# Filler matmuls on TensorE while the convolution's matrices are built

## The chip, the cores and the metric

The kernel runs on one core of one Trainium2 chip. Its time is the device time of one execution in microseconds (us), taken as the median over several executions. Five engines work side by side: TensorE (PE in the profile, with its weight loads as PEld), VectorE (DVE), ScalarE (ACT), GpSimd (POOL) and SyncE (SP), which here issues most of the DMAs. Matmul results land in PSUM, eight banks of 2 KB per partition. TensorE's clock is throttled by the chip: the profile shows the granted clock as a share of full speed, and in this kernel it is always either 1.0 or 0.5.

## The reference

Two independent parts are joined on the last axis. Part A is a recurrent memory attention over 64 segments of 32 rows, part B a state-space convolution (S4 form) over 2048 positions and 1024 channels:

```python
a = _A_ref(A_x, A_mem0, A_Wq, A_Wk, A_Wv, A_Wo, A_seg_len)     # 64 segments, one after the other
# part B, for each channel d:
P = jnp.exp(logdA[:, :, None] * l[None, None, :])              # powers of the state, l = 0 .. 2047
K = jnp.einsum('dn,dnl,dn->dl', Cc, P, dB).real                # the convolution's kernel
Kf, Uf = rfft2(pad(K)), rfft2(pad(u))                          # length 4096
y = irfft2(Uf * Kf)[..., :L] + u * Dskip
return jnp.concatenate([a, y], axis=-1)
```

## The kernel before, in words

Part B comes first (roughly the first 590 us), then part A (the remaining 1350 us); loads of part A's weights are already issued during part B. The order of the work is written out by hand (`manual_schedule`): each engine runs its instructions in the order in which the program issues them, and waits only where data or a buffer demand it.

Part B has three stages. First, 16 passes (lines 1325 to 1360) compute samples of the convolution's kernel K, transform u into the frequency domain (kept in DRAM as `Ud`), and make part A's projections. Then comes the stage that the change touches, lines 1367 to 1423 and the blocks 0 to 3 of the loop at line 1526. Last come the blocks 4 to 15 of that loop, with the inverse transforms.

In the touched stage K's spectrum is needed, and for it matrices of cosines and sines are built. There are four of them (`G[kc]`, kc = 0 to 3), each made in 14 steps by the generator `build` (line 1179):

- One step makes the basis: a matmul with 7 rows by 7 columns, moving 512 elements (line 1190), then a sine on ACT.
- Ten steps make angles: two matmuls with 7 rows and 128 columns, 256 elements each, into one bank (line 1186), then a sine of 512 elements per partition on ACT (line 1177).
- Three steps make weights: one matmul with 7 rows and 512 elements (line 1198), then a copy on ACT (line 1199).

Every step takes a PSUM bank (named `gf`) from a pool of three, which the tiles `kp` use too. `make(kc, n)` (line 1369) runs n of the steps. `weighted(kc, n_)` (line 1205) multiplies three of the five angle blocks of one half of `G[kc]` by the weights, on DVE. `spectrum(b, n_)` (line 1217) is 20 matmuls of 128 rows and 128 columns, 256 elements each, into a tile of two banks: `pa` for blocks 0 to 3, `hps` later. `times_u` (line 1377, operation at line 1380) multiplies the spectrum by u's, on DVE, and `rotate` (1383, 1384) ends the complex product. `values(15, t)` (line 1063) are the last small matmuls for K, into two of the three `gf` banks; `table_ops["x"]` (line 1071) copies them out on DVE.

PE's order in the touched stage is: 9 steps of `make(0)`; 3 more; `spectrum(0, 0)`; 2 more; `spectrum(0, 1)`; 9 steps of `make(1)`; `values(15, 0)` and `values(15, 1)`; 5 more steps; `spectrum(1, 0)`; `spectrum(1, 1)`; 14 steps of `make(2)`. Then in block 1 of the loop `spectrum(2, 0)`, 7 steps of `make(3)`, `spectrum(2, 1)` and 7 steps; in block 2 the two halves of `spectrum(3)`; in block 3 those of `spectrum(4)`. At the start of block 3 the PSUM pools are closed and two new ones are opened, `ps_h` for the tiles `hps` and `ps_y` for the tiles `yp` of the inverse transforms. `load_u(b)` (line 1215) issues on SP the two loads `wq<-Ud` for block b; they wait until DVE has read the buffers they overwrite. `inverses` (lines 1506 to 1521) end with a store on ACT's queue, `out_dram<-uu`.

Two other names are needed: `ps_t` (line 998) is the pool of one bank that held the tiles `ptt` of the first stage, and `Dsk` (line 735) is a constant of 128 x 1024 in bf16, loaded in the eighth of the 16 passes (line 1327) and used by DVE at line 1486.

Of the kernel before, what the change touches and what calls it, by code (L numbers as in the profile page):

```python
# [11 lines left out]
F32 = mybir.dt.float32  # L12
# [675 lines left out]

COARSE = [(16, 32, 16), (544, 64, 8), (1088, 128, 8)]
FINE = [(-64, 8, 4), (-32, 4, 4), (-16, 1, 32), (16, 4, 4), (32, 8, 5)]  # L690
TURNS = [(0, 1, 17), (20, 4, 4), (40, 8, 4)]
NC, NP, NN, NA = 32, 25, 24, 25
STEP, CENTER, ONE = 16, 192.0, 120
# [18 lines left out]
def part_b(ctx, tc, u, A_re, A_im, B_re, B_im, C_re, C_im, log_dt, Dskip, out_b, ahead, copies, residents, first_state):  # L712
# [6 lines left out]
    v, sc, gp, pe, sy = nc.vector, nc.scalar, nc.gpsimd, nc.tensor, nc.sync  # L719
# [15 lines left out]
    Dsk = const.tile([128, D], BF16, name="Dsk")  # L735
# [41 lines left out]
    with tc.tile_pool(name="b_par", bufs=1) as par, tc.tile_pool(name="b_parh", bufs=2) as parh, \  # L777
# [35 lines left out]
        o = 0  # L813
        for b0, st, n in FINE + COARSE + TURNS:
            gp.iota(jI[:, o:o + n], pattern=[[st, n]], base=b0, channel_multiplier=0)
# [152 lines left out]
        for word_ in PAR:  # L968
            word = word_.rstrip("/")
            nm, n_ = word[0], word[1:]  # L970
# [27 lines left out]
    ps_t = ctx_p.enter_context(tc.tile_pool(name="b_pst", bufs=1, space=PSUM))  # L998
# [206 lines left out]
    def weighted(kc, n_, amp):  # L1205
        a_ = amp.rearrange("p (j q) -> p j q", j=3)[:, :, 256 * n_:256 * n_ + 256]
        g_ = G[kc][:, n_, 2:5].rearrange("p j s h f -> p j s (h f)")
        v.tensor_tensor(out=g_, in0=g_, in1=a_.unsqueeze(2).to_broadcast([128, 3, 2, 256]), op=ALU.mult)
# [4 lines left out]
    def load_u(b):  # L1213
        for n_ in range(2):
            sy.dma_start(out=uq[n_], in_=Ud[b % 4, b // 4][:, 2 * n_:2 * n_ + 2].rearrange("p a c d -> p (a c d)"))

    def spectrum(b, n_, outs, halves=(0, 1)):
        dq, kc = b // 4, b % 4
        KT = ks[dq // 2]
        d = slice(DQ * (dq % 2), DQ * (dq % 2) + DQ)  # L1220
        for half in halves:
            for cs in range(2):
                for j in range(5):
                    pe.matmul(outs[half][:, cs, :], lhsT=G[kc][:, n_, j, cs, half, :], rhs=KT[j][:, d], start=(j == 0), stop=(j == 4), skip_group_check=True)  # L1224
# [57 lines left out]
    def cosine(r, h):  # L1282
        sc.activation(out=cosines(r, h), in_=T["n", r, h][:], func=ACT.Sin, scale=-TWO_PI, bias=hp[:])

    def minus(r, h):
        wn = T["w", r, h] = tmp.tile([128, 32, NN], BF16, name="wn", tag="wn", bufs=1)
        v.tensor_scalar(out=wn[:], in0=turned(windows(T["s", r, h])), scalar1=-1.0, scalar2=None, op0=ALU.mult)

    def imaginary(r, h):
        products(r, h, "gi", windows(T.pop(("s", r, h))), T.pop(("w", r, h))[:])  # L1290

    def real(r, h):
        c_ = cosines(r, h).rearrange("p (a b) -> p a b", a=32)
        products(r, h, "gr", c_, turned(c_))

    def values(r, t):
        T["K", r, t] = part(r, t, [T["gr", r, h] for h in range(2)], [T["gi", r, h] for h in range(2)])
# [68 lines left out]

    made = [build(kc, lambda: take([128, 512], F32, "gf"), amps[kc]) for kc in range(4)]

    def make(kc, n):
        for _ in range(n):  # L1370
            next(made[kc])

    def halves():
        t_ = ps_e.tile([128, 2, 512], F32, name="pa", tag="pa")
        return [t_[:].rearrange("p h (c d) -> p h c d", c=2)]
# [9 lines left out]
    now = [halves() for _ in range(2)]  # L1385
    first = XT[:, 15360:19456].bitcast(F32).rearrange("p (a b c d) -> p a b c d", a=2, b=2, c=2)
    zs = [up.tile([128, 2, 2, DQ], F32, name="us", tag="us", bufs=3) for n_ in range(2)]
    absolute(15, 0)
    minus(15, 0)
    make(0, 9)  # L1390
    imaginary(15, 0)
    absolute(15, 1)
    minus(15, 1)
    imaginary(15, 1)
    make(0, 3)
    weighted(0, 0, amps[0])
    spectrum(0, 0, [now[0][0][:, half] for half in range(2)])
    make(0, 2)
    weighted(0, 1, amps[0])
    spectrum(0, 1, [now[1][0][:, half] for half in range(2)])  # L1400
    cosine(15, 0)
    cosine(15, 1)
# [3 lines left out]
    load_u(1)  # L1406
    real(15, 1)
    make(1, 9)
    for t in range(2):
        values(15, t)  # L1410
    make(1, 5)
# [40 lines left out]
    def pointwise(b, s_):  # L1452
        kc, Bt = b % 4, Bs[b // 4]
        Y = Yp[:] if b else first
        whole = b > 3
        if b:
            for n_ in range(2):
                times_u(s_, Y[:, n_], Zs[:, n_], n_)
                if n_ == 0 and not whole:
                    rotate(Y[:, n_], Zs[:, n_])  # L1460
        yield
        if whole:
            rotate(Y.rearrange("p n a c d -> p (n a) c d"), Zs[:].rearrange("p n a c d -> p (n a) c d"))
        elif b:
            rotate(Y[:, 1], Zs[:, 1])
        v.tensor_tensor(out=even, in0=Y[:, 0], in1=Y[:, 1], op=ALU.add)
        v.tensor_tensor(out=odd[:], in0=Y[:, 0], in1=Y[:, 1], op=ALU.subtract)
        for i, op in ((0, ALU.add), (1, ALU.subtract)):
            gp.tensor_tensor(out=Bt[:, kc, 0, i], in0=even[:, 0], in1=even[:, 1], op=op)
        eng, to = v if b == 15 else gp, blocks(Bt[:, kc, 1])  # L1470
        eng.tensor_tensor(out=to[:, 0:4:3], in0=odd[:, 0], in1=odd[:, 1, ::-1], op=ALU.add)
        eng.tensor_tensor(out=to[:, 2:0:-1], in0=odd[:, 0], in1=odd[:, 1, ::-1], op=ALU.subtract)
# [10 lines left out]
    def skips(n_):  # L1483
        d = slice(DQ * (n_ // 4), DQ * (n_ // 4) + DQ)
        uu = held[n_][:].rearrange("p i a d -> p (i a) d")
        v.tensor_tensor(out=uu, in0=uu, in1=Dsk[:, d].unsqueeze(1).to_broadcast([128, 4, DQ]), op=ALU.mult)
# [39 lines left out]
    for b in range(16):  # L1526
        dq = b // 4
        if b % 4 == 0:
            Bs[dq] = (bp0, bp)[dq % 2].tile([128, 4, 2, 2, 2, DQ], BF16, name="Bt", tag="B")
        points = pointwise(b, now)  # L1530
        next(points)
        if b >= 4:
            skips(b - 4)
        if 0 < b < 15:
            load_u(b + 1)
        if b >= 4:
            load_pair(b - 2, iv)
        if b == 3:
            v.tensor_scalar(out=ident[:], in0=ident[:], scalar1=float(PLEN / 2), scalar2=None, op0=ALU.mult)
            load_pair(0, iv)  # L1540
            load_pair(1, iv)
            ctx_p.close()
            ctx_k.close()
            ps_h = ctx.enter_context(tc.tile_pool(name="b_psh", bufs=3, space=PSUM))
            ps_y = ctx.enter_context(tc.tile_pool(name="b_psy", bufs=2, space=PSUM))
        if b == 0:
            now = nxt_
        elif b + 1 < 16:
            now = []
            for n_ in range(2):  # L1550
                if b < 3:
                    if n_:
                        next(points, None)
                    weighted(b + 1, n_, amps[b + 1])
                now.append(halves() if b < 3 else [ps_h.tile([128, 2, 2, DQ], F32, name="hps", tag="h")[:]])
                spectrum(b + 1, n_, [now[n_][0][:, half] for half in range(2)])
                if b == 1:
                    make(3, 7)
        next(points, None)
        if b < 4:  # L1560
            for i in (2 * b, 2 * b + 1):
                sy.dma_start(out=MI[i][:], in_=MId[2 * i:2 * i + 2].rearrange("c p a k q -> p c a k q"))
        if b == 2:
            rows4 = g0[0:4, 5120:6144]
            for i in range(4):
                for half in range(2):
                    sy.dma_start(out=rows4[i:i + 1, DH * half:DH * half + DH], in_=Kx[half][31:32, NF - 1].rearrange("i g c -> i (g c)"))
            sy.dma_start(out=w4, in_=u[0:4, :])
            gp.tensor_tensor(out=w4, in0=rows4[:, 0:D], in1=w4, op=ALU.mult)
            gp.memset(l4, 0.0)  # L1570
            gp.memset(l4[:, :, 127:128], float(PLEN / 2))
            gp.affine_select(out=l4[:, :, 127:128], in_=l4[:, :, 127:128], compare_op=ALU.is_ge, fill=0.0, base=0, pattern=[[1, 4], [0, 1]],
                             channel_multiplier=-1)
        for _ in range({1: 2, 2: 2, 3: 1, 4: 2, 5: 2, 6: 2, 7: 2, 11: 3, 12: 3, 13: 2, 14: 3, 15: 3}.get(b, 0)):
            next(resident)
        for _ in range(4 if b in (3, 4) else 0):
            second.pop(0)()
        if b == 5:
            ks.append(load_k(1, k1[:, 0:2560], 0))
        if b == 4:  # L1580
            state = first_state(g0[0:8, 5120:6144], iv.tile([128, 8, 24], BF16, name="xt0", bufs=1))
            next(state)
        if b == 10:
            state.send(ps_y.tile([128, 8, 128], BF16, name="yp", tag="yp")[:, :, 0:8])
        if b >= 4:
            for i in range(2):
                inverses(b - 4, i)
# [178 lines left out]
```

## Time and profile before

| | |
|---|---|
| median of 3 runs | 1939.64 us (1933.28 to 1943.44) |
| the profiled execution: time | 1942.13 us |
| the profiled execution: span | 1940.4 us, mean granted clock 0.974 |
| PE busy over the span | 1783.4 us (92%) |
| DVE busy | 1356.6 us (70%) |
| ACT busy | 918.6 us (47%) |
| 374 to 443 us (the touched stage): PE, DVE, ACT busy of 69 us | 54.87, 58.10, 35.16 us |
| the same stretch: granted clock, DMA share | 0.67, 0.71 |
| 620 to 1900 us (most of part A): granted clock, DMA share | 1.00, 0.96 |

Times in the trace are counted from the start of the span. "Busy" counts an engine's instructions, not how full they are; matmuls overlap, so that a row such as "4.50 us, x20" with the next row starting 4.44 us later means 0.222 us from one matmul to the next. Where the profile says that an instruction was idle before, it names what ended the wait.

### The profile page before, as it was taken

To read this page: it belongs to the slowest core of one execution; us is meant where nothing else is said; L and a number is where in the kernel's file an instruction comes from. 1 tells how busy PE (TensorE), PEld (TensorE's weight loads), DVE (VectorE), ACT (ScalarE), POOL (GpSimd) and SP (SyncE) were. 2 spreads that over 40 slices of the span, in tenths; PEclk is the share of its full clock that TensorE was granted. 3 is DMA by queue.
4 is the path that set the end of the run, shared out by engine and by line. 5 is a ranking of instruction groups with operands and counts; after the bars stand their busy time and mean duration, and the time that the engine had idled before them with its cause. 6 is when DMAs were issued, how large, how long until landed. Compare 5 with 4: busy or idle time off the path is not lost.

```text
span 1940.4 us, 73670 instructions
## 1 busy us (share of the span) xinstructions
PE 1783.4 (92%) x31563; PEld 1091.3 (56%) x31563; DVE 1356.6 (70%) x3357; ACT 918.6 (47%) x1654; POOL 499.4 (26%) x885
## 2 busy tenths in 40 slices
PE   8999999888886999999999999999999999999998
PEld 3666565556763555555555555555555555555554
DVE  8699999798992666676666666666667666766650
ACT  8799999850112343444444443434344444434420
POOL 2364545236561111111111111111112121111120
PEclk9999999868997999999999999999999999999999
DMA  7889898868699999999999999999999999999993
GB/s 222 250 238 282 238 282 250 216 193 249 196 294 373 334 336 341 339 342 342 340 339 349 344 335 340 346 339 344 331 349 343 343 343 357 336 337 339 345 338 96
DMA packets 341744, 594.21 MB, mean 306 GB/s; under 512 B 94100, under 2 KB 216476, under 8 KB 339368
## 3 DMA queue, kind: packets, MB, share of 16 engines
q1 hardware_dynamic: 297944, 534.99, 81.4%
q10 hardware_dynamic: 36816, 29.59, 4.8%
q0 software_dynamic: 6656, 24.92, 3.4%
q8 instruction: 247, 4.05, 0.8%
q14 instruction: 81, 0.66, 0.1%
HBM read 531.92 MB, written 71.63 MB: 311 GB/s over the span
## 4 chain that ended last, share of the span: by engine, by line
PE 46%; DMA 33%; DVE 12%; ACT 5%; issue 2%; POOL 1%; ACTq 0%; SPq 0%; POOLq 0%; DVEq 0%
PE acc L414 19%; DMA wst<-WD_v 12%; DMA wst<-WD_o 9%; PE pp L527 8%; DMA arena<-PKd 4%; PE pe L667 3%; DMA wst<-WD_k 3%; DMA wst<-WD_q 2%; PE tr L425 2%; PE pro L184 2%; PE yp L1508 1%; DVE nr L1269 1%; PE hps L1224 1%; PE pro L197 1%; PE pa L1224 1%
## 5 line engine op out<-in xcount | busy, mean ns | idle before, releaser
L414 PEld LDWEIGHTS <-a_hT 128*32 128x32 bf16 x12351 | 327.9, 96 | 331.5 <-issue 80.5
L420 ACT CAST arena<-acc 128x512 bf16<-128x512 f32 x384 | 224.8, 585 | 406.0 <-PE acc L414 336.8
L414 PE MATMUL acc<-wst,a_hT 128*32 128x512 bf16 x2308 | 230.5, 383 | 36.6 <-DMA wst<-WD_v 27.1
L527 PEld LDWEIGHTS <-arena 128*32 128x32 bf16 x8256 | 215.3, 96 | 76.7 <-issue 52.6
L428 POOL COPY arena<-arena 128x128 bf16<-128x128 bf16 x128 | 37.4, 292 | 707.1 <-DMA arena<-PKd 343.8
L335 DVE TENSOR_SCALAR arena<-keep 128x256 int32<-128x256 int32 x508 | 174.1, 394 | 26.6 <-PE acc L414 26.6
L414 PE MATMUL acc<-XM,a_hT 128*32 128x512 bf16 x2560 | 173.4, 381 | 0.0
L454 DVE TENSOR_REDUCE a_mx<-sc 128x4 f32<-128x160 f32 (+1 forms) x192 | 71.7, 374 | 80.9 <-PE sc L442 80.8
L197 PE MATMUL pro<-XM,wsl 128*128 128x512 bf16 x512 | 122.4, 382 | 4.0 <-DVE kst L206 2.2
L527 PE MATMUL pp<-W_o,arena 128*32 128x256 bf16 x3584 | 121.2, 273 | 1.3 <-issue 1.3
L414 PE MATMUL acc<-W,a_hT 128*32 128x512 bf16 x1536 | 119.7, 384 | 0.0
L544 DVE COPY arena<-tr 128x512 bf16<-128x512 bf16 x64 | 27.2, 424 | 129.2 <-PE tr L425 129.2
L458 ACT ACTIVATE sc<-sc 128x160 f32<-128x160 f32 (+1 forms) x192 | 63.9, 333 | 103.3 <-DVE sc L455 102.7
L462 DVE TENSOR_REDUCE a_mx<-sc 128x4 f32<-128x160 f32 (+1 forms) x192 | 72.8, 379 | 55.2 <-ACT sc L458 54.9
L489 POOL TENSOR_TENSOR arena<-arena,a_BD 128x128 bf16<-128x128 bf16 x128 | 51.0, 399 | 213.6 <-DVE arena L472 203.0
L1269 DVE TENSOR_SCALAR nr<-ptt 128x456 f32<-128x456 int16 x128 | 80.2, 627 | 30.4 <-PE ptt L1247 27.4
L1261 ACT ACTIVATE E<-pa 128x648 bf16<-128x648 f32 x128 | 87.6, 712 | 17.0 <-PE pa L1253 15.4
L414 PE MATMUL acc<-wq,a_hT 128*32 128x512 bf16 x1024 | 92.3, 383 | 0.0
L527 PE MATMUL pp<-wst,arena 128*32 128x256 bf16 x1536 | 76.2, 274 | 17.5 <-DMA wst<-WD_o 16.5
L414 PE MATMUL acc<-g,a_hT 128*32 128x512 bf16 x1024 | 91.2, 380 | 0.0
L623 ACT CAST arena<-pp 128x128 bf16<-128x128 f32 x64 | 17.0, 265 | 155.7 <-DVE arena L623 155.7
L513 ACT CAST arena<-pv 128x512 bf16<-128x512 f32 (+1 forms) x128 | 61.3, 479 | 60.3 <-PE pv L499 33.3
(342 smaller groups left out, 4001.7 us busy)
## 6 DMA issues: line engine op xcount, KB each, us to landing
wst<-WD_v SPq DMA_DIRECT2D x256, 512.0 KB
wst<-WD_k SPq DMA_DIRECT2D x192, 512.0 KB
wst<-WD_o SPq DMA_DIRECT2D x192, 512.0 KB
wst<-WD_q SPq DMA_DIRECT2D x128, 512.0 KB
Ud<-ux POOLq DMA_DIRECT2D x16, 1024.0 KB, 8.9
wq<-Ud SPq DMA_DIRECT2D x32, 512.0 KB
wsl<-in_A_Wk_dram SPq DMA_DIRECT2D x16, 512.0 KB
wsl<-in_A_Wv_dram SPq DMA_DIRECT2D x16, 512.0 KB
```

Source lines behind the costliest of these rows:

```text
L197: nc.tensor.matmul(a[:], lhsT=w[:, kc, 128 * j:128 * j + 128], rhs=xTl[:, kc, :, :].rearrange("p s k -> p (s k)"), start=(kc == 0), stop=( ...
L335: nc.vector.tensor_scalar(out=out.bitcast(I32), in0=in_.bitcast(I32), scalar1=0, scalar2=None, op0=ALU.bitwise_or)
L414: nc.tensor.matmul(a[32 * g:32 * g + 32, o_:o_ + rhs.shape[1]], lhsT=hT[:, kc, :], rhs=rhs, start=(kc == 0), stop=(kc == KC - 1), tile_pos ...
L420: nc.scalar.copy(out=q, in_=a[:])
L454: nc.vector.tensor_reduce(out=m_, in_=x, axis=AX.X, op=ALU.max)
L458: nc.scalar.activation(out=flat(sc, i), in_=flat(sc, i), func=ACT.Exp, scale=scale)
L462: nc.vector.tensor_reduce(out=m_, in_=x, axis=AX.X, op=ALU.add)
L513: copy(out=o[:, i:i + n], in_=p[:, i:i + n, :].rearrange("p a (g q) -> p a g q", g=4))
L527: nc.tensor.matmul(po[32 * qt:32 * qt + 32, o_:o_ + rhs.shape[1]], lhsT=oT[:, h % 4, (h % 16) // 4, :], rhs=rhs, start=False, stop=(h == 3 ...
L667: nc.tensor.matmul(pe[n][:], lhsT=left[2 * b + hi // 16][:, 128 * (hi % 16):128 * (hi % 16) + 128], rhs=wo[u][:, 1024 * hh + 512 * n:1024 ...
L1261: sc.activation(out=T["E", r, e // 4][:, lo:lo + 8 * NE].rearrange("p (i c) -> p i c", i=2), in_=T.pop(("p", r, e))[:, :, 0:4 * NE], func= ...
L1269: v.tensor_scalar(out=T["n", r, e // 4][:, lo:lo + 8 * NT], in0=T.pop(("t", r, e))[:, 0:8 * NT].bitcast(I16)[:, 0:16 * NT:2], scalar1=floa ...
```

## The change

A function `keep_busy(t_, n)` issues n matmuls of 128 rows, 128 columns and 512 elements, all from the constant `Dsk`, into a bank that nobody reads. Each `make` step is followed by one of them, and further ones stand at eight places. The bank is first one half of the first `pa` tile (its real contents are written later), then the bank of `ps_t`, and from block 3 on a tile of `ps_y`. Counted through the program there are 103 such matmuls: of the 56 `make` steps 55 are followed by one and one (the third of `make(0)`) by 6, which makes 61; 9 + 3 + 7 + 5 = 24 stand between the calls before the loop; and 18 stand ahead of `spectrum(2, 0)`, `(3, 0)`, `(3, 1)` and `(4, 1)`. Apart from them, the order of the instructions on PE, DVE, ACT, POOL and SP is the same in both programs.

```diff
+WAITS = {(2, 0): 3, (3, 0): 5, (3, 1): 6, (4, 1): 4}
...
-    def make(kc, n):
+    def keep_busy(t_, n):
         for _ in range(n):
+            pe.matmul(t_, lhsT=Dsk[:, 0:128], rhs=Dsk[:, 0:512], start=True, stop=True, skip_group_check=True)
+
+    def make(kc, n, more=()):
+        for i in range(n):
             next(made[kc])
+            keep_busy(idle_, 6 if i in more else 1)
...
-    make(0, 9)
+    idle_ = now[0][0][:, 0].rearrange("p c d -> p (c d)")
+    keep_busy(idle_, 9)
+    make(0, 9, (2,))
     imaginary(15, 0)
...
     make(0, 3)
+    idle_ = ps_t.tile([128, 512], F32, name="ptt", tag="ptt")[:]
+    keep_busy(idle_, 3)
     weighted(0, 0, amps[0])
     spectrum(0, 0, [now[0][0][:, half] for half in range(2)])
     make(0, 2)
     weighted(0, 1, amps[0])
+    keep_busy(idle_, 7)
     spectrum(0, 1, [now[1][0][:, half] for half in range(2)])
...
     make(1, 9)
+    keep_busy(idle_, 5)
     for t in range(2):
         values(15, t)
...
             ps_y = ctx.enter_context(tc.tile_pool(name="b_psy", bufs=2, space=PSUM))
+            idle_ = ps_y.tile([128, 512], F32, name="yp", tag="yp")[:]
...
                 now.append(halves() if b < 3 else [ps_h.tile([128, 2, 2, DQ], F32, name="hps", tag="h")[:]])
+                keep_busy(idle_, WAITS.get((b + 1, n_), 0))
                 spectrum(b + 1, n_, [now[n_][0][:, half] for half in range(2)])
```

## The prediction

> **What bounds the stage now.** I read the slices of the span first, then the waits of DVE in the touched stretch, then the clock in single stretches, then the chain behind it.
>
> ```profile
> PE   8999999888886999999999999999999999999998
> DVE  8699999798992666676666666666667666766650
> PEclk9999999868997999999999999999999999999999
> ```
>
> Each digit is 48.5 us. The granted clock is low only in the eighth to eleventh slice and the thirteenth: from 340 to 534 us it shows 8, 6, 8, 9. DVE is near full in the same slices. Which of the two paces the stage is seen in DVE's waits from 374 to 445 us:
>
> ```profile
> DVE g L1208 <- ACT g L1177: 5.6, 1, 5.6
> DVE XM L1208 <- ACT XM L1177: 1.8, 1, 1.8
> DVE g L1208 <- ACT wq L1199: 0.9, 1, 0.9
> DVE XM L1208 <- ACT wq L1199: 0.8, 1, 0.8
> DVE z L1380 <- issue: 0.6, 1, 0.6
> DVE nr L1280 <- ACT sn L1274: 0.6, 1, 0.6
> DVE z L1380 <- PE pa L1224: 0.4, 1, 0.4
> ```
>
> Together 10.7 us. DVE works without a break otherwise, so the stage cannot end more than 10.7 us (0.55% of the time) earlier however fast PE is. That is the ceiling of this change up to 443 us.
>
> The next answer counts only the matmuls of line 1224 (128 rows); columns are PE busy, PEld busy, clock, DMA share, GB/s. The stretches are 3.41 us long, which is the step of the clock's changes in this trace.
>
> ```profile
> 387.34:390.76 3.42, 1.33 (x11) 0.96 (x12) 1.00 0.70 148
> ...
> 411.24:414.65 3.41, 0.00 (x0) 0.00 (x0) 1.00 0.93 261
> 414.65:418.06 3.41, 1.67 (x8) 1.16 (x9) 0.50 0.87 311
> 418.06:421.48 3.42, 2.77 (x13) 1.62 (x11) 0.50 0.95 304
> 421.48:424.89 3.41, 1.13 (x11) 1.02 (x12) 1.00 0.87 344
> ...
> 435.13:438.54 3.41, 2.24 (x19) 1.67 (x18) 1.00 0.24 68
> 438.54:441.96 3.42, 0.00 (x0) 0.00 (x0) 1.00 0.95 309
> 441.96:445.37 3.41, 2.39 (x12) 1.72 (x13) 0.50 0.71 205
> ```
>
> And all of PE, DVE, ACT, POOL in one of them:
>
> ```profile
> 411.24:414.65 3.41, 2.69 (x13) 1.07 (x12) 3.41 (x4) 3.41 (x8) 1.49 (x1) 1.00 0.93 261
> ```
>
> The reader is to see a rule. At full clock, a stretch with 1.33 us or less of 128-row matmuls is followed by half clock (387, 421, 411), one with 2.24 us keeps it (435). At half clock, 1.67 or 2.39 us are not enough to return (414, 441), 2.77 us are (418). From 411 PE was busy 2.69 of 3.41 us with the 7-row matmuls of `build`, and the clock still fell.
>
> By the Trainium skill ("TensorE: Matmul & The Clock Gate", section "Why this matters for your kernels") it is enough to have no PE-idle gap over about 3 us between bursts. By that rule the clock would not have fallen here, and only the 4.78 us gap before 443 us would cost anything, which no filler covers. The trace disagrees: busy 2.69 us with 7 rows, clock lost.
>
> Behind the stage the chain runs through PE and a store:
>
> ```profile
> 440.66 1.13 DVE z L1380
> 441.79 1.14 DVE y L1380
> 442.94 0.05 issue
> 442.98 11.72 PE hps L1224 x80
> ...
> 468.22 5.54 DMA out_dram<-uu
> 473.77 1.23 SPq L1098
> ...
> 475.10 9.84 DMA wq<-Ud
> ```
>
> **Prices.** A filler is 512 elements. Nearest rows: at full clock `pro` L197, eight of 512 take 1.72 us from first start to the next group (337.57 to 339.29), 0.215 each; at half clock spectrum(0, 0), 20 of 256 from 382.79 to 387.23, 0.222 each, so 0.43 for 512. The 103 fillers are 22 us of PE at full clock, 44 at half. PE is idle 69 - 54.87 = 14.1 us of the stretch, and 54 us of it ran at half clock.
>
> Will they hold the clock? In `make`, ACT needs 0.49 us a step (L1177: six in 2.95). One filler a step is 0.215 / 0.49 = 44%, or 1.5 us of each 3.41. That lies between 1.33 (lost) and 2.24 (kept). Counted by streaming in the same way, the stretches 387 and 421 that lost the clock had 11 matmuls of 256, 11 x 0.108 = 1.18 us. Elsewhere the stretch 69.87 to 73.28 kept it with six matmuls of 324 elements and two of 456 whole (2856 x 0.215 / 512 = 1.20 us) and, at its ends, up to 0.27 us of two groups that reach into it. So 1.5 us lies above everything that lost it and above one that kept it: I take the clock as held, narrowly.
>
> The fillers' banks add no wait: ACT's last read of `pa` ends at 372.56, DVE's last of `ptt` at 375.02, both before the first filler into that bank.
>
> **The walk, with the clock held.** Times before, then after.
>
> 1. Nine fillers (1.9 us) after 374.2 lie in PE's wait of 1.79 us for ACT (376.00), six (1.3 us) in that of 1.56 us (378.48). ACT then runs without a break to 383.67, as before: no change. The 0.6 and 0.9 us waits of DVE stay.
> 2. The last angle before spectrum(0, 0) needs the bank that ACT's third copy frees at 382.22. Angle 0.22, four fillers 0.86: the spectrum starts at 383.3 (before 382.79), and its 20 matmuls take 20 x 0.108 = 2.16 instead of 4.44: it ends at 385.5 (387.23). Two sines behind it end at 387.0 (388.78). DVE's weighted(0, 1) starts 1.8 us earlier. The seven fillers end at 387.6, before weighted(0, 1) does at 387.9, and delay nobody.
> 3. spectrum(0, 1) ends at 389.9 (392.9), so the sines and copies of `make(1)` follow the cosine without ACT's wait of 1.42 us. weighted(1, 0) is ready when DVE is: the 0.78 us wait goes. Total 2.6.
> 4. The five fillers lie before `values`, which wait for DVE. The last three angles of `make(1)` still wait until DVE empties the `kp` banks (402.01 before, 399.4 after), then 0.25 us of matmul and three sines, 1.57: DVE's 1.81 us wait becomes 1.4. Total 3.0.
> 5. spectrum(1, 0) and (1, 1) end at 404.6 (410.0); with one lost clock window between, 406.7. The 0.40 us wait goes: 3.4.
> 6. Blocks 1 to 3: DVE is continuous, PE has fillers in slots where it waits for `weighted`. spectrum(2, 1) ends at 420.7 against a need at 423.2 (before 427.1, the 0.64 us wait): that goes too. Total 4.0 at 443 us.
> 7. PE still waits about 4.8 us for DVE ahead of spectrum(4, 0), so half clock returns there; four fillers between its halves cost 0.86 to 1.7 us on the path shown above. Against it, the half-clock part was 5.8 us of the 7.2 us there (the clock rose at 448.78); with another place in the 3.41 us grid it lasts 2.5 to 5.9 us, on average 4.2, which gives back (5.8 - 4.2) / 2 = 0.8. I set -0.1: total 3.9, bounds 2.3 to 5.
>
> The sequences of DMAs on SP and of POOL's adds are not touched; SP's `wq<-Ud` waits mostly for DVE (72.8 us in 23 waits from 380 to 600 us), so they move with it. The two later waits of DVE for `wq<-Ud` (3.52 and 3.44 us at 471.71 and 485.03) hang on the chain above and stay. From 486 to 570 us DVE is busy 82.75 of 84 us: it carries the gain on. Part A's DMA share is 0.96 throughout, its pace is its own; what starts earlier ends earlier.
>
> The sum: -3.9 us against the profiled 1942.13, that is 1938.2. That execution lies 2.5 above the median of 1939.64, from which I forecast 1935.7. Ends: with the chain of step 7 at its bounds and step 2 to 6 each off by one wait, -2 to -7.
>
> **Rivals.**
>
> *The fillers do not hold the clock, and PE becomes the bound (slower).* Decided by whether 1.5 us of 3.41 suffices; the rows at 387 and 421 us speak for it, the stretch at 69.87 against. It is a trap, because at half clock a step is 0.43 + 0.49 = 0.92 us, of which the filler's 47% are 1.6 us per 3.41, less than the 2.39 that did not restore it. PE would then need 54.9 + 99 x 0.43 = 97 us for the 69 us stretch, +28; if the spectra restore half of it, 99 x 0.32 instead, +18. I take +20: about 1960. A fall in one `make` of 14 steps alone costs 14 x 0.43 = 6 us, minus the 2 to 4 us slack of step 6.
>
> The Trainium skill ("TensorE: Matmul & The Clock Gate", section "Why this matters for your kernels"), by its rule of gaps, would give this direction too: where the 7-row matmuls already count as busy, fillers between them change no clock and only add their own time.
>
> *The gain is lost at the hand-over.* From 570 to 620 us the DMA share is 0.97 at 347 GB/s, loads of part A's weights. If these are bounded by bandwidth since before 570, an earlier end of part B only waits for them: 1939.6 plus or minus the run spread of 4. Against it: from 486 to 570 the share is 0.76, and SP waits for DVE and stores.
>
> *More goes than DVE's few waits.* If ACT's small chains of steps 2 and 4 shrink to nothing and the half-clock stretch at 474 us goes as well, up to 10.7 + 1 us: 1928 to 1930. Nothing in PE's order says so, since the bank and the order of sines stay.
>
> **Numbers.** Forecast 65%, hand-over 17%, clock not held 10%, more 8%. Single executions spread 10 us, so a median can be off by 3. A difference under 0.5% (9.7 us) is what this kernel cannot tell from no change. Faster by more: the 8%, and 4 points from the forecast's edge, 0.12. Slower by more: the 10%, 0.1. Between: 0.78. The range takes the forecast's -7 and the run spread below, and the hand-over and a partial loss of the clock above: 1929 to 1945.
>
> **What would show it.** Granted clock near 1.0 from 374 to 434 us (0.67 from 374 to 443 before), DVE's 5.6 us wait at about 3.8, those of 0.8, 0.4 and 0.6 gone, and block 4's first `hps` matmul near 439. Wrong, if half clock stands in `make` stretches (fillers 0.43 apart), if ACT waits for PE there, or if the first `acc` matmul of part A (593 before) does not start 3 to 4 us earlier.

## The result, and the profile after

The changed kernel takes 1945.94 us (median of 22 runs, 1937.43 to 1956.03), the kernel before 1938.09 us (median of 22 runs, 1924.99 to 1947.9). The ratio is 1.0035 with a 95% interval of 1.002 to 1.0051. The change makes the kernel slower by about 7 us; 1935.7 us had been forecast, 4 us faster, with a range of 1929 to 1945. The measured time lies just above that range. The profiled execution took 1947.67 us with a span of 1946.0 us.

The slices of the span after the change, of 48.6 us each:

```profile
PE   8999999898886999999999999999999999999998
DVE  9699999779992666666666666676766566666650
PEclk9999999889998999999999999999999999999999
```

The ninth slice, 389 to 438 us, has changed most: the clock there rose from 6 to 8 and PE from 8 to 9, but DVE fell from 9 to 7. The granted clock from 374 to 400 us rose from 0.63 to 0.89, and from 400 to 443 us from 0.70 to 0.83, but PE is busy for 69.00 of these 69 us (54.87 before), while DVE's busy time there fell from 58.10 to 47.07. The waits of DVE from 374 to 445 us say what it now waits for:

```profile
DVE g L1209 <- ACT g L1178: 6.7, 1, 6.7
DVE z L1386 <- PE pa L1225: 3.8, 1, 3.8
DVE XM L1209 <- ACT XM L1178: 3.4, 2, 2.6
DVE z L1386 <- issue: 3.0, 1, 3.0
DVE XM L1209 <- ACT wq L1200: 2.3, 1, 2.3
DVE g L1209 <- ACT wq L1200: 2.0, 1, 2.0
DVE nr L1281 <- ACT sn L1275: 0.6, 1, 0.6
```

In all 21.8 us, where it was 10.7. (Lines are one higher than before: 1178 is the sine, 1200 the copy of weights, 1209 `weighted`, 1187 the angles, 1225 the spectrum; 1372 is the filler.)

Where the loss arises is seen by following one DVE instruction after the other in both traces: the start after minus the start before, each from the start of its span. It is -0.01 us at 380.77 us, +1.06 us at 382.26 (`weighted(0, 0)`), +2.14 at 388.81 (`weighted(0, 1)`), +3.66 at 401.88, +7.19 at 423.00, +8.52 at 442.96, +6.65 at 485.03 and +7.25 at 575.41, the end of part B. Part A begins with its first `acc` matmul at 600.21 instead of 593.16 us. So the loss is made in the touched stage, and most of it arrives at the end: +5.5 us at 1935 us in this execution, 1.0035 as the ratio over all runs. The first 1.06 us of it arise at full clock, since the granted clock was 1.00 from 370.29 to 383.95 us.

PE's timeline in the first steps of `make(0)` shows what costs it. The columns are start, length, and then the instruction:

```profile
376.71 0.39 PE L1187 MATMUL gf<-g,XM 7*128 7x256 bf16 x2
377.03 0.39 PE L1372 MATMUL pa<-Dsk 128*128 128x512 bf16 x1
377.35 0.39 PE L1187 MATMUL gf<-g,XM 7*128 7x256 bf16 x2
377.67 1.47 PE L1372 MATMUL pa<-Dsk 128*128 128x512 bf16 x6
379.07 0.39 PE L1187 MATMUL gf<-g,XM 7*128 7x256 bf16 x2
```

A single filler takes 0.32 us (377.03 to 377.35) and so does the pair of angles (376.71 to 377.03). Six fillers in a row take 1.40 us (377.67 to 379.07), that is five of 0.215 and one of 0.32. Only the filler that is followed by a 7-row matmul is dearer, by 0.107 us, and so is the 7-row pair that is followed by a filler (two of 256 elements are 0.215 otherwise). One step is then 0.64 us long, and ACT needs 0.49. The weight loads in the same stretch:

```profile
376.71 0.11 PEld L1187 LDWEIGHTS <-XM 7*128 7x128 bf16 x2 [0.23 <-issue]
377.02 0.10 PEld L1372 LDWEIGHTS <-Dsk 128*128 128x128 bf16 x1 [0.21 <-issue]
377.35 0.11 PEld L1187 LDWEIGHTS <-XM 7*128 7x128 bf16 x2 [0.23 <-issue]
```

The filler's load starts at 377.02, when the angles ahead of it have streamed and the filler itself is recorded to start (377.03). A single load takes 0.09 to 0.10 us (the 0.11 is a pair), which is about the surcharge. ACT has become the slower for it:

```profile
377.85 3.53 ACT L1178 ACTIVATE g<-gf 7x512 bf16<-7x512 int16 x6
381.42 1.86 ACT L1200 CAST wq<-gf 128x512 bf16<-128x512 f32 x3
```

Six sines take 3.53 us where they took 2.95, three copies 1.86 where they took 1.51. And the clock is not held. In the stretches of 3.41 us (columns: PE, PEld, DVE, ACT, POOL busy, clock, DMA share, GB/s), the steps of `make(1)` and of `make(2)`:

```profile
394.19:397.60 3.41, 3.41 (x17) 1.10 (x16) 3.41 (x4) 2.90 (x6) 0.00 (x0) 1.00 0.42 154
397.60:401.01 3.41, 3.41 (x8) 0.61 (x6) 1.89 (x3) 1.97 (x4) 0.00 (x0) 0.50 0.45 151
...
414.67:418.08 3.41, 3.41 (x15) 1.01 (x13) 3.41 (x4) 3.18 (x6) 3.01 (x2) 1.00 0.98 242
418.08:421.49 3.41, 3.41 (x11) 0.75 (x10) 3.38 (x5) 1.92 (x5) 0.00 (x0) 0.50 0.93 319
```

PE is busy without a break and yet the clock falls. A filler of 0.215 us in a step of 0.64 is a third of the time: counted by streaming, 128-row matmuls fill 0.31 of the stretch at 394.19 and 0.33 of that at 414.67. At half clock a step takes 1.07 us (filler 0.54, angles 0.54), more than twice ACT's 0.49.

The chain of work behind the stage has kept its form. Block 4's first matmul is at 451.50 (442.98 before); the four fillers stand between its halves:

```profile
451.50 3.81 PE hps L1225 x20
455.30 1.08 PE yp L1372 x4
456.39 6.55 PE hps L1225 x60
```

These 11.4 us with the fillers take the place of 11.72 without. From 442.96 to 485.03 us the shift falls from 8.52 to 6.65, but the matmuls give back only 0.3 us of that: it is 8.24 at 460.45 and still 8.05 at 471.71. The last 1.4 us come at DVE's second wait for `wq<-Ud`, which is 2.04 us long and was 3.44.

### The profile page after: what moved, and what is told of

Same layout as the page of the kernel before. It is cut to its first block, busy times and chain, and to the rows that moved or that the text cites. A ratio compares the mean times of both kernels' runs of the same rounds, so it can differ in the third digit from the quotient of the medians.

```text
span 1946.0 us, 73876 instructions
## 1 busy us (share of the span) xinstructions
PE 1801.7 (93%) x31666; PEld 1093.4 (56%) x31666; DVE 1354.8 (70%) x3357; ACT 924.5 (48%) x1654; POOL 501.9 (26%) x885
## 4 chain that ended last, share of the span: by engine, by line
PE 47%; DMA 32%; DVE 14%; ACT 3%; issue 3%; POOL 1%; SPq 0%; DVEq 0%; POOLq 0%; ACTq 0%
PE acc L414 21%; DMA wst<-WD_v 11%; PE pp L527 7%; DMA wst<-WD_o 7%; DMA wst<-WD_k 5%; DMA wst<-WD_q 3%; PE pe L667 3%; PE tr L425 2%; DVE nr L1270 2%; DMA arena<-PKd 2%; PE pro L184 1%; PE yp L1520 1%; PE hps L1225 1%; PE ptt L1372 1%; DVE gr L1236 1%
## 5 line engine op out<-in xcount | busy, mean ns | idle before, releaser
L425 PEld LDWEIGHTS <-arena 128*128 128x128 bf16 x1024 | 57.8, 98 | 54.8 <-issue 26.3
```

Of the source, the lines that this page charges most:

```text
L425: nc.tensor.transpose(out=p[:, hl, :, :].rearrange("p a b -> p (a b)"), in_=q[:, 128 * hl:128 * hl + 128], identity=ident[:])
```

## The experiments

Four theories stand at the start. Theory S: a filler inside a step costs PE 0.43 us instead of 0.215, as the weight load is uncovered at each change between 7 and 128 rows, and PE becomes the bound. Beside it stand theory O (the fillers outside the steps delay the spectra), theory K (only the lost clock costs time) and theory P (a filler costs 0.43 us for another reason). The shifts below are worked out as above, from one profiled execution each, at four places of the trace of before: at 350 us (ahead of everything that is touched), at 380.77, at 442.96 and at 485.03 us. What a kernel adds in the stage is the difference of the last and the second of them. For the two kernels that have two traces, it comes out within 0.7 us.

| kernel | 350 | 380.77 | 442.96 | 485.03 | clock 374-400 / 400-443 | ratio to before, 95% |
|---|---|---|---|---|---|---|
| the change | -0.04 | -0.01 | +8.52 | +6.65 | 0.89 / 0.83 | 1.0035 (1.002 to 1.0051) |
| outside_only | +0.13 | -0.68 | -1.08 | +0.56 | 0.80 / 0.76 | 1.0001 (0.9977 to 1.0025) |
| steps_only | +4.95 | +4.12 | +19.43 | +17.63 | 0.67 / 0.72 | 1.0078 (1.0054 to 1.0103) |
| two_a_step | +0.68 | +0.54 | +13.43 | +11.22 | 1.00 / 1.00 | 1.0079 (1.0049 to 1.0109) |
| seven_rows | +0.92 | +0.76 | +8.85 | +6.93 | 0.80 / 0.72 | 1.002 (0.9991 to 1.0048) |
| full_rows | +0.04 | +0.70 | -4.27 | -4.28 | 0.87 / 0.84 | 0.9997 (0.9972 to 1.0022) |
| full_rows_103 | -0.10 | +0.53 | -3.29 | -4.25 | 1.00 / 0.91 | 1.0 (0.9976 to 1.0024) |

### The fillers outside the steps alone, and those inside alone

```diff
     def make(kc, n, more=()):
         for i in range(n):
             next(made[kc])
-            keep_busy(idle_, 6 if i in more else 1)
```

> The changed kernel without its fillers inside the steps of `make`; the 42 fillers outside stay. Theory S (a filler inside a step costs PE 0.43 us instead of 0.215, because each change between a 7-row and a 128-row matmul leaves about 0.107 us of weight load uncovered; PE becomes the bound of the steps): the steps go back to ACT's pace, six sines in about 2.95 us (3.53 in the changed kernel) wherever the clock was full, DVE's start of `weighted(0, 0)` returns to 382.3 us, and at 485 us DVE stands within 2 us of before, not 6.65 us later. Time ratio to before 0.999 to 1.001. Rival O (the fillers outside, in front of the spectra and the `kp` tiles, are what delays): the loss stays, DVE 5 to 8 us later than before at 485 us, ratio 1.003 to 1.004.

In `steps_only` every other call of `keep_busy` is taken out:

```diff
-            keep_busy(idle_, 6 if i in more else 1)
+            keep_busy(idle_, 1)
...
-    keep_busy(idle_, 9)
```

> The reverse: one filler in each step of `make` (56), none outside. Theory S: the loss of the changed kernel stays, 5 to 8 us at 485 us, steps 0.64 us apart at full clock and 1.07 us at half clock, ratio 1.003 to 1.004. Rival O: the loss goes, DVE within 2 us of before at 485 us, ratio 0.999 to 1.001. If both kernels lose about half, both theories are parts of the cause.

With the fillers outside alone the loss is gone (1.0001). PE's timeline shows the steps at ACT's pace again, three of angles from 377.79 to 379.22 and three of weights to 380.64, 0.48 us each:

```profile
377.79 1.53 PE L1187 MATMUL gf<-g,XM 7*128 7x256 bf16 x6 [1.48 <-ACT g L1178]
379.22 1.53 PE L1199 MATMUL gf<-g 7*128 7x512 bf16 x3
380.64 1.53 PE L1187 MATMUL gf<-g,XM 7*128 7x256 bf16 x6
```

With the fillers inside alone it is there, and larger than expected: between 380.77 and 485.03 us the shift grows by 13.5 us, twice the 6.65 of the change. Theory O falls. That it is twice as much is a miss of the expectation. The clock is 0.67 and 0.72 there against 0.89 and 0.83, so the fillers outside had helped: with them the clock stays up for longer (also without any inside, 0.80 and 0.76 against 0.63 and 0.70 before), and at full clock a step costs 0.64 and not 1.07 us. A stretch at full clock in this kernel, which lost it:

```profile
404.34 0.39 PE L1372 MATMUL ptt<-Dsk 128*128 128x512 bf16 x1
...
406.26 0.39 PE L1372 MATMUL ptt<-Dsk 128*128 128x512 bf16 x1
406.58 0.39 PE L1187 MATMUL gf<-g,XM 7*128 7x256 bf16 x2
406.90 0.61 PE L1372 MATMUL ptt<-Dsk 128*128 128x512 bf16 x1
407.44 0.60 PE L1199 MATMUL gf<-g 7*128 7x512 bf16 x1
```

From the filler at 404.34 to that at 406.26 are three steps of 0.64 us; at 406.90 the clock is halved, and the filler takes 0.54 (to 407.44).

### Two fillers in each step: clock held, time lost

```diff
-            keep_busy(idle_, 6 if i in more else 1)
+            keep_busy(idle_, 6 if i in more else 2)
```

> The changed kernel with two fillers in each step of `make` (six at one place as before). The 128-row share of a step becomes 0.43 / 0.855 = 0.50 at full clock. Theory S: the clock is held from 374 to 437 us, better than in the changed kernel, and yet the stage is not faster, since a step takes 0.855 us against ACT's 0.49: 56 steps add 56 x 0.36 = 20 us of PE, of which the slack of DVE and PE hides about half: DVE 6 to 14 us later than before at 443 us, ratio 1.003 to 1.007. Rival K (only the lost clock costs time): with the clock held, DVE stands 3 to 4 us earlier than before at 443 us, ratio below 1.

The clock is 1.00 throughout the stage, and the kernel is slower still:

```profile
374.00:400.00 26.00, 25.82 (x162) 10.46 (x149) 15.63 (x20) 18.40 (x26) 1.12 (x3) 1.00 0.65 174
400.00:443.00 43.00, 42.09 (x349) 17.44 (x347) 30.42 (x33) 21.20 (x36) 13.28 (x8) 1.00 0.55 166
```

ACT waits for PE in every step, which is 0.855 us long (381.33 to 382.18):

```profile
381.33 0.60 ACT L1178 ACTIVATE g<-gf 128x512 bf16<-128x512 int16 x1 [0.26 <-PE gf L1187]
382.18 0.60 ACT L1178 ACTIVATE g<-gf 128x512 bf16<-128x512 int16 x1 [0.26 <-PE gf L1187]
```

Theory K falls: with the clock fully held, PE's time per step alone makes the stage 10.7 us longer (0.54 to 11.22). The ratio, 1.0079, is a little above the 1.003 to 1.007 that were expected.

### Fillers of 7 rows: no change of rows inside a step

```diff
-    def keep_busy(t_, n):
+    def keep_busy(t_, n, rows=128):
...
-            pe.matmul(t_, lhsT=Dsk[:, 0:128], rhs=Dsk[:, 0:512], ...)
+            pe.matmul(t_, lhsT=Dsk[0:rows, 0:128], rhs=Dsk[0:rows, 0:512], ...)
```

In `make`, `rows` is 7.

> The changed kernel with its fillers inside `make` cut to 7 rows, of the same 512 columns: the same count and the same streaming, but no change of rows inside a step. Theory S: at full clock filler and step follow each other at 0.215 us and a step takes ACT's 0.49 us; since 7 rows hold no clock, half clock comes as in the kernel before or more, and there a step takes 0.86 us: DVE 5 to 15 us later than before at 485 us. Rival P: at full clock a step still takes 0.64 us.

The same count and streaming, and the surcharge is gone (377.38 to 377.60 and 377.60 to 377.82, 0.22 each, at full clock):

```profile
377.38 0.38 PE L1187 MATMUL gf<-g,XM 7*128 7x256 bf16 x2
377.60 0.37 PE L1372 MATMUL pa<-Dsk 7*128 7x512 bf16 x1
377.82 0.38 PE L1187 MATMUL gf<-g,XM 7*128 7x256 bf16 x2
```

So it is the change of rows that costs the angles and the filler 0.107 us, and not the change of bank or operand. These fillers do not hold the clock: 7-row matmuls streamed for 3.35 us of the stretch from 377.68 to 381.09, and half clock followed. At half clock a step is 0.86 us, and the shift grows by 6.2 us to 485.03, inside what was expected. That is nearly the 6.7 us of the change. So without the surcharge, fillers that do not hold the clock cost about as much; how the loss of the change divides between the surcharge and the half clock behind it is not shown, beyond its first 1.06 us.

### Full rows without fillers

The 7-row matmuls of `build` get the whole array by operands of 128 rows, of which 121 are zero in the moving one; the products do not change.

```diff
-            G.update({0: part_of(g0, 0), "rhs": g0[0:7, 5120:7168], "wts": g0[0:7, 7168:7552], "basis": g0[0:7, 7552:8064], "lhs": XT[0:7, 2048:3456]})
+            G.update({0: part_of(g0, 0), "rhs": g0[:, 5120:7168], "wts": g0[:, 7168:7552], "basis": g0[:, 7552:8064], "lhs": XT[:, 2048:3456]})
+            gp.memset(g0[:, 5120:8064], 0.0)
...
-                copy(out=G["lhs"][:, 0:1024], in_=flat)
+                copy(out=G["lhs"][0:7, 0:1024], in_=flat)
```

The other copies and the basis's sine write rows 0 to 6 in the same way.

> The kernel before, without fillers, but with the operands of the 7-row matmuls of `build` extended to 128 rows by zeros (the products do not change); one memset on POOL more. Theory R (the clock counts rows, so the 7-row matmuls are what loses it): a step has 0.215 us of 128-row matmul in ACT's 0.49 us, 44%, above the 0.38 to 0.39 of a 3.41 us stretch that kept full clock in the changed kernel, so the clock stays near 1.0 from 374 to 437 us (0.67 before) at no extra matmul; DVE's 5.6 us wait falls to about 3.8, those of 0.8, 0.6 and 0.4 go, and DVE stands 3 to 4 us earlier than before at 443 us; ratio 0.997 to 0.999. Rival C (the zero rows do not count, or the share is still too small): half clock at the same places as before, no shift, ratio 0.999 to 1.001.

The clock rises to 0.87 and 0.84, with no matmul more than before. Rival C falls: zero rows count for the clock. It is not held everywhere; up to 435 us, half clock stands at 376.7 to 383.5, 400.6 to 404.0 and 424.5 to 431.3 us, and in the stretch ahead of each 128-row matmuls streamed for 0.11, 0.28 and 0.32 of the time, since `make` had paused there. Stretches with 0.44 and 0.46 kept it, which is the 44% of ACT's pace. DVE's waits from 374 to 445 us:

```profile
DVE g L1208 <- ACT g L1177: 3.6, 1, 3.6
DVE XM L1208 <- ACT XM L1177: 1.6, 1, 1.6
DVE g L1208 <- ACT wq L1199: 0.9, 1, 0.9
```

The 5.6 us wait is 3.6, and those of 0.8, 0.6 (`z`) and 0.4 us are gone, as expected. The stage is 5.0 us shorter (+0.70 to -4.28). The time is not shown to follow (0.9997).

### Full rows with all the fillers

The changed kernel with the same edit.

> The changed kernel with all its 103 fillers, and the operands of the 7-row matmuls extended to 128 rows by zeros. Theory S: with 128 rows on both sides of each filler the uncovered weight load goes; filler and step follow each other at 0.215 us each, 0.43 us a step, below ACT's 0.49, six sines take 2.95 us again, the clock stays near 1.0, and DVE stands 3 to 4 us earlier than before at 443 us, which is what the prediction walked through; ratio 0.997 to 0.999. Rival P (a filler costs 0.43 us for another reason, such as the change of bank or of operand): steps stay 0.64 us apart, DVE 3 us later than before or worse, ratio 1.001 or above.

This is the change with the surcharge taken out. The edit does a second thing as well: the matmuls of `build` now count for the clock themselves, so that 128-row matmuls fill 0.43 of a step's 0.49 us and not only the filler's 0.215. The prediction's "held, narrowly" is thus not tested here; `full_rows`, with 0.44 at ACT's pace, tests that. PE's timeline and weight loads:

```profile
377.37 0.38 PE L1373 MATMUL pa<-Dsk 128*128 128x512 bf16 x1
377.58 0.38 PE L1187 MATMUL gf<-g,XM 128*128 128x256 bf16 x2
377.80 1.46 PE L1373 MATMUL pa<-Dsk 128*128 128x512 bf16 x6
```

```profile
377.26 0.10 PEld L1373 LDWEIGHTS <-Dsk 128*128 128x128 bf16 x1
377.37 0.31 PEld L1187 LDWEIGHTS <-XM 128*128 128x128 bf16 x2
```

Filler and angles follow each other at 0.215 us, and the loads run while the matmul before them streams (the filler's load at 377.26 lies beside the angles of 377.15). ACT's six sines are back at 2.95:

```profile
378.38 2.95 ACT L1178 ACTIVATE g<-gf 7x512 bf16<-7x512 int16 x6
381.24 1.51 ACT L1200 CAST wq<-gf 128x512 bf16<-128x512 f32 x3
```

The clock is 1.00 from 374 to 400.9 us. Theory P falls, S stands. Counted from 380.77 us, the shift goes to -1.73 at 388.81 (the prediction's step 2: -1.8), -2.6 at 401.88 (steps 3 and 4: -2.6 to -3.0), -3.1 at 423.00 and -3.8 at 442.96 (step 6: -4.0), and -4.8 at 485.03 (step 7: -3.9). `full_rows`, without a single filler, comes to -5.0 there. With the wider operands the 103 fillers add nothing to the gain of the stage.

### Does a gain of the stage reach the end?

Neither `full_rows` nor `full_rows_103` is faster, though their traces are 4 us ahead at 575 us. `full_rows` also starts the stage 0.7 us late: ACT's copy of `rhs` (idle 2.21 us ahead of it) starts at 363.12, as the memset ends that ran from 360.54; before, it started at 360.77. Further kernels have the memset in three pieces:

```diff
-            gp.memset(g0[:, 5120:8064], 0.0)
+            for at, end in ((5120, 6144), (6144, 7168), (7168, 8064)):
+                gp.memset(g0[:, at:end], 0.0)
```

`full_rows_split` is `full_rows` with that, run twice; `full_rows_103_split` has all fillers too; `full_rows_103_again` repeats the kernel above. `best` has the 42 fillers outside the steps, and 16 more in block 3:

```diff
+            keep_busy(idle_, 16)
             ctx_p.close()
             ctx_k.close()
```

> The kernel with 128-row operands in `build` and without any filler, with the memset in three pieces. The 0.7 us that the stage started later goes: DVE 4.5 to 5.5 us earlier than before at 485 us. If what the stage gains reaches the end: ratio 0.997 to 0.998. If part A does not take it up: 0.999 to 1.001.

> The kernel with 128-row operands in `build`, no filler inside the steps, the 42 fillers outside of them, 16 more after spectrum(3, 1) in PE's wait of 4.78 us for DVE ahead of block 4, and the memset in three pieces, so that ACT's first copy waits for 1024 columns of it and not for 2944. If the losses are the ones named (clock, change of rows, memset): DVE 5 to 6 us earlier than before at 443 us, full clock from 438 on, which takes up to 3 us from the chain of block 4's matmuls, and 6 to 9 us earlier at 485 us. If what the stage gains reaches the end: ratio 0.995 to 0.997. If part A does not take it up: 0.999 to 1.001.

> The same kernel as full_rows_103, for more runs. If its 4 us at 485 us reach the end: ratio 0.997 to 0.999; if part A does not take them up: 1.000 again, as in the first twelve runs.

> The same kernel as full_rows_split, for more runs: its stage was 7 us shorter than before's, and its ratio 0.998. If that gain reaches the end, 0.996 to 0.999 again; if the first twelve runs were a chance, 0.999 to 1.001.

> The kernel with 128-row operands, all 103 fillers, and the memset in three pieces, beside full_rows_split on the same chip. Its stage should be 4.5 to 7 us shorter than before's from 380 to 485 us. If a stage's gain reaches the end whatever made it: ratio 0.996 to 0.999, as without fillers. If the fillers cost something behind the stage, so that 24 runs of full_rows_103 showed no gain: 0.9995 to 1.001.

| kernel | 350 | 380.77 | 442.96 | 485.03 | end (1935) | ratio to before, 95% |
|---|---|---|---|---|---|---|
| full_rows_split | +4.45 | +3.66 | -1.31 | -3.47 | -9.2 | 0.9978 (0.9961 to 0.9995) |
| full_rows_split_again | +3.82 | +3.03 | -1.94 | -3.45 | -10.5 | 0.9986 (0.9966 to 1.0006) |
| best | +3.98 | +2.89 | -1.80 | -2.09 | -10.4 | 0.9986 (0.9967 to 1.0004) |
| full_rows_103_again | -0.05 | +1.84 | -1.81 | -3.26 | -0.1 | 1.0013 (0.9992 to 1.0034) |
| full_rows_103_split | +2.20 | +1.98 | -1.01 | -1.78 | -9.7 | 0.9997 (0.9974 to 1.0019) |

The stage is shorter in each of them, by 3.8 to 7.1 us from 380.77 to 485.03. `full_rows_103_split`, with 3.8, stays below the 4.5 to 7 us expected of it. Four kernels, `steps_only` among them, come to the stage 2 to 5 us late already (the column 350), through work ahead of it that no edit touches. The clock says why. In `steps_only` it falls to 0.50 from 75.80 to 79.22 us, and once more from 280.60 to 284.02. `best` and both traces of `full_rows_split` lose it in the same way at 74 to 76 and at 279 to 281 us; before, it is 1.00 throughout from 18.7 to 363.5 us. The shift grows by about 1.5 us over the first of these places and by 1.1 over the second. Up to 1 us more comes from a later first rise of the clock (23.8 to 24.6 us, 18.7 before), in `full_rows_103_split` too, which loses it at neither place. The clock changes in steps of 3.41 us, and these steps lie elsewhere in each trace: in `steps_only` the stretch from 72.39 holds 0.32 of 128-row matmuls, while before, the stretch from 69.87 reaches 0.43 (the prediction's 1.20 and 0.27 us). So such a delay can come with an execution; it is not shown to belong to a kernel. It hides part of the gain at 485 us. `full_rows_split` is the only version whose interval lies below 1, in one of its two sets, and the second set points the same way. As one in seven sets with 128-row operands it may be chance. Taken as it stands, it is ahead of the changed kernel (1.0035), and of the kernel before by some 0.2%.

`best` missed its expectation. Its clock is 1.00 and 0.96, but what block 4 gained (the shift goes from -1.80 at 442.96 to -3.15 at 460.45 us) turned into a longer wait of DVE for the transfers (-0.93 at 471.71). The wait from 374 to 490 us:

```profile
DVE z L1387 <- DMA wq<-Ud: 8.0, 2, 5.7
```

Before, these two waits were 3.52 and 3.44 us; here they are 5.74 and 2.28. So a faster chain there only waits longer for `wq<-Ud`.

Whether a gain of 3 to 5 us reaches the end is left open. The losses of the stage did arrive (+6.65 us as 1.0035, which is 6.8 us; +17.6 as 1.0078, 15 us; +11.2 as 1.0079, 15 us). But part A moves by itself: `outside_only` is +0.54 us at 575 us and -10.2 at the end. Against that, `full_rows_103` showed no gain in two sets of executions, and `full_rows_split`, with about the same shift at 485 us, showed some in two; the traces do not say why.

## Why the prediction was wrong

The step that failed is the term "prices": "a filler is 512 elements ... 0.215 each" and, from it, "one filler a step is 0.215 / 0.49 = 44%". The 0.215 us came from `pro`, 128 rows behind 128 rows. In a step the filler stands between 7-row matmuls, and there it costs 0.43 us at full clock: its own 0.215 and two changes of rows of 0.107. The step becomes 0.215 + 0.215 + 2 x 0.107 = 0.64 us, longer than ACT's 0.49, and PE the bound. The trace of before had a row for it, in part B's inverse transforms, where a 4-row matmul stands between 128-row ones. PE's timeline of the kernel before:

```profile
590.78 1.69 PE L1508 MATMUL yp<-Bt,MI 128*128 128x256 bf16 x14
592.41 0.28 PE L1506 MATMUL yp<-k 4*128 4x256 bf16 x1
592.62 0.39 PE L1508 MATMUL yp<-Bt,MI 128*128 128x256 bf16 x2
592.85 0.38 PE L1520 MATMUL yp<-uu,b_ident 128*128 128x512 bf16 x1
```

The 4-row matmul has 256 elements, and the next starts 0.21 us later instead of 0.108; the 14 ahead of it take 1.63 us, 0.12 more than 14 x 0.108. The prediction priced the filler by its own shape alone and took no row in which the shape changes.

- *Will they hold the clock?* The forecast of "held, narrowly" fell with the same term: 1.5 us of 3.41 became 1.1 us, as the step is longer, and that is less than the 1.18 us that the prediction itself had seen lose the clock. The reading of the clock was not at fault: 0.44 and 0.46 of a stretch kept it in `full_rows`, and 0.31 to 0.34 lost it in the changed kernel.
- *Step 1* (fillers lie in PE's waits, "ACT then runs without a break ... no change") failed first: the nine fillers fit, but the steps behind them set ACT's pace, six sines in 3.53 us.
- *Steps 2 to 7* hold where their condition holds. In `full_rows_103`, without the surcharge and with a clock that the wider operands help to hold, they come out within about 1 us each.
- *The rival "PE becomes the bound"* named the direction, and its +20 us was too large by a factor of three for the change, as the fillers outside brought the clock back between the steps. For `steps_only`, which lacks these, 13.5 us came out. Its condition was wrong: it hung on the clock alone, and `two_a_step` shows that the loss comes with the clock held too. Its step of 0.92 us at half clock adds PE's filler to ACT's 0.49; by the prediction's own prices PE's step is 0.43 + 0.43, and 1.07 was measured.
- *The hand-over*: the losses were carried into part A; for the gains it stayed open. "What starts earlier ends earlier" is not shown.
- *The rule of gaps.* The Trainium skill ("TensorE: Matmul & The Clock Gate", section "Why this matters for your kernels") wants no PE-idle gap over about 3 us. The trace disagrees again: the stretch at 394.19 had PE busy for all 3.41 us and lost the clock.
- *A slip without consequence:* 54 us of the stage were said to run at half clock. A mean clock of 0.67 over 69 us makes it 45 us; nothing in the sum uses it.

## What to carry to other kernels

Price an inserted instruction by a row in which its neighbours are those it will have, not by a row of equals: here the change of shape doubled its price. And work out the step of the loop with it before asking about any second effect: a step that the insertion makes longer than the engine it feeds is lost even where the clock is won. Where the narrow matmuls themselves are the reason for a low clock, giving them the whole array with zero rows did more than matmuls beside them.

## What the runs showed of the hardware

- A change between a matmul of 7 (or 4) rows and one of 128 rows costs 0.107 us at full clock: the weight load, 0.09 to 0.10 us, starts only when the matmul ahead of it has streamed. Between 128 and 128 rows, and between 7 and 7, it is hidden (0.215 to 0.22 us for 512 elements). At half clock a filler between 7-row matmuls took 0.54 us instead of 0.43, the same 0.107 more. The Trainium skill ("TensorE: Matmul & The Clock Gate", section "The mechanism") says that weight loads overlap matmuls in flight only when the row groups differ. The measurement differs: here they overlap where the rows are the same and do not where 7 follow 128, and it decides. The same section also lets a load that goes to a background weight buffer run ahead of matmuls in flight; no run here shows where a load goes.
- A change of columns cost as much. In `full_rows_103` the basis matmul of `make(0)` has 128 rows like the fillers beside it, but 7 columns. Its load starts at 376.61 us, 0.31 us after the filler ahead of it (0.215 between fillers), and the next filler starts 0.31 us later. In `make(1)` (407.80 to 408.11) it is 0.31 again.
- The clock counted rows that hold zeros: with 128-row operands, of which 121 rows are zero, and no other matmul, it rose from 0.63 to 0.87 (374 to 400 us). With 7 rows, 3.35 us of matmul in a stretch (`seven_rows`, from 377.68) did not keep it.
- In the thirteen traces of these kernels, from 20 to 600 us, every stretch at full clock in which 128-row matmuls of 128 columns streamed for more than 0.39 of the 3.41 us kept the clock; the most that lost it was 0.39 (`full_rows_split`, from 427.15). Where neither 32-column nor 96-row matmuls ran beside them, the least that kept it was 0.33 (`seven_rows`, from 394.74), with 7-row matmuls for 0.60 more. Between 0.33 and 0.39 some stretches kept it and some lost it. The prediction's 0.44 (1.5 us) was rightly taken as enough.
